# Staging v of three batches through a scratch tensor in HBM, so that its transposes run in float32r

## The chip, the cores and the metric

The kernel runs on one core of a Trainium2 chip. The metric is the device time of one execution in microseconds (us); shown is the median of several runs. One further execution was recorded by the hardware profiler, and all rows below come from it.

## What is computed

The input is four batches of q, k and v, each of 5056 tokens by 256 channels. Attention runs over channels: the score matrix of a batch is 256x256, and its result, 20224 rows of 256, goes through a mixture of eight experts, of which each row takes one.

```python
# attention, one batch
qn = q / (np.linalg.norm(q, axis=1, keepdims=True) + 1e-06)
kn = k / (np.linalg.norm(k, axis=1, keepdims=True) + 1e-06)
a = softmax(kn.transpose(0, 2, 1) @ qn / tau)      # 256 x 256
x = v @ a
# experts, all rows
logits = x @ w_gate + modality_bias[modality_id]
e_idx = np.argmax(logits, axis=1)
h = np.maximum(x[mask] @ w1[e], 0.0)               # 256 -> 1024
out[mask] = gate_w[mask, None] * (h @ w2[e])       # 1024 -> 256
```

## The kernel before

Every float32 product is made of three float32r matmuls: an operand is split into a high part, which is its float32r rounding, and a low part, the rest.

A batch is cut into ten steps of 512 tokens (the last has 448), which makes 40 steps, numbered g = 0 to 39. A step of the main loop (from L726 on) mixes up to three streams of pieces, evenly, by `_interleave` (L20): a block of 512 rows of one expert (`hp` is its first product, L629, and `y` its second, L645; there are blocks from step 7 on), the attention's own stream, and, but for the last batch, the scores of the next batch (`g`, L270 and L274). So the work of about one block, one v step and one score step lies interleaved on every engine.

The attention's stream of step g is `load`, `tr(0)` and `tr(1)` of step g+1, and then `av(0)` to `av(3)` and `route` of step g:

- `load` (L419) takes one of two buffers for v and fills it by a DMA that SyncE issues (L424). Row p of a partition holds four successive tokens.
- `tr(h)` (L434) transposes half of the channels: four TensorE transposes of 128x128 (L440, `vtp`) into one PSUM bank, which ScalarE then copies to the high part `vh` (L444) and VectorE turns into the low part `vl` (L445). v is float32 there, and so are the identity `ident` and the PSUM tile.
- `av(t)` (L447) forms 128 rows of x (L456, `xp`), six matmuls each. `route` (L463) finds each row's expert and scatters the rows by GpSimd into `xs`, a tensor in HBM (L388).

A block loads its rows of `xs` into `xr` (L559) and transposes them by `tr_x` (L605). That one differs from `tr`: `xr` is a float32r tile, filled through a float32 view, and its four transposes (L611, `xtp`) use `identr`, the float32r identity, into a float32r PSUM tile.

Nobody writes an order of engines by hand: the pieces are emitted in the order of the mix, TensorE runs in that order, and on the other engines an instruction whose inputs are ready may be placed ahead of earlier ones. `setup_bias(b+1)` is such a piece: it is emitted after step 5 of a batch, and it begins with two DMAs that load `modi` (L176 and L180), which depend on nothing but a free buffer.

Of the kernel before, what the change touches and what calls it, by code (L numbers as in the profile page):

```python
# [8 lines left out]
F32 = mybir.dt.float32  # L9
F32R = mybir.dt.float32r  # L10
# [3 lines left out]
ALU = mybir.AluOpType  # L14
# [3 lines left out]


def _interleave(*streams):  # L20
    """Emit the pieces of several generators, evenly mixed."""
    lists = [list(s) for s in streams if s]
    total = [len(x) for x in lists]
    at = [0] * len(lists)
    while any(a < n for a, n in zip(at, total)):
        i = min(
            (i for i in range(len(lists)) if at[i] < total[i]),
            key=lambda i: ((at[i] + 0.5) / total[i], i),
        )
        lists[i][at[i]]()  # L30
        at[i] += 1
# [3 lines left out]
def kernel(  # L35
# [13 lines left out]
    nc = tc.nc  # L49
    P = 128  # L50
    B, N, C = q.shape
    T, D = out.shape
    E, _, FF = w1.shape
    TT = 4
    STEP = P * TT
    NS = -(-N // STEP)
    G = B * NS
# [13 lines left out]
    START = 3  # L71
# [6 lines left out]
    p2 = ctx.enter_context(tc.tile_pool(name="p2", bufs=2))  # L78
# [3 lines left out]
    ps1 = ctx.enter_context(tc.tile_pool(name="ps1", bufs=1, space=PSUM))  # L82
    ps2 = ctx.enter_context(tc.tile_pool(name="ps2", bufs=2, space=PSUM))

    # ---- constants
    ident = const.tile([P, P], F32, name="ident")
    make_identity(nc, ident)
    identr = const.tile([P, P], F32R, name="identr")
# [29 lines left out]
    nc.vector.tensor_scalar(desc, iof, -1.0, float(E), ALU.mult, ALU.add)  # L118
    base0 = const.tile([P, E], F32, name="base0")
    nc.vector.tensor_scalar(base0, iof, float(CAP), None, ALU.mult)  # L120
    # the ninth column is the spare region, taken only when no expert has a block left
    eid9 = const.tile([1, E + 1], F32, name="eid9")
    nc.vector.memset(eid9, 0.0)
    nc.vector.tensor_copy(eid9[:, 0:E], iof[0:1, :])
# [10 lines left out]
    nc.vector.memset(end9, float(E * CAP + BLK))  # L135

    xs = dram.tile([ROWS, XW], F32, name="xs")
    pad = const.tile([P, XW], F32, name="pad")
    nc.gpsimd.memset(pad, 0.0)
    nc.gpsimd.memset(pad[:, D + 1 : D + 2].bitcast(I32), BADTOK)  # L140
# [58 lines left out]
        )  # L199
        nc.gpsimd.tensor_tensor(bs, bs, tmp, ALU.add)  # L200

    # ---- scores of one batch, a step of tokens at a time
    gram = {}
    acc = {}
    selfk = {}
# [2 lines left out]
    def kq_pieces(b, s):  # L208
        pp = parts(s)
        st = {}  # L210
# [52 lines left out]
        def mm(h):  # L263
            qs, ks = st[h]
            for t in range(2):
                first = s == 0 and h == 0 and t == 0
                last = s == NS - 1 and h == 1 and t == 1
                for m in range(CH):
                    g = gram[b][m]
                    nc.tensor.matmul(  # L270
                        g, ks[:pp, t, m * P : (m + 1) * P], qs[:pp, t, :],
                        start=first, stop=False, skip_group_check=True,
                    )
                    nc.tensor.matmul(  # L274
                        g[:, 0:C], ks[:pp, t, C + m * P : C + (m + 1) * P], qs[:pp, t, 0:C],
                        start=False, stop=last, skip_group_check=True,
                    )
                    if s < SELF[b]:
                        nc.tensor.matmul(  # L279
                            selfk[b][:, m, :], ks[:pp, t, m * P : (m + 1) * P],  # L280
                            ks[:pp, t, :].rearrange("p (s c) -> p s c", s=2)[:, :, m * P : (m + 1) * P],
                            start=first and m == 0, stop=s == SELF[b] - 1 and h == 1 and t == 1,
                            skip_group_check=True,
                        )
            if s == SELF[b] - 1 and h == 1:
                # the diagonal of k'k, from its high parts with themselves and with the low ones, twice
                dg = p1.tile([P, 2 * P], F32, tag="sc", name=f"dg_{b}", bufs=2)
                normk[b] = p1.tile([P, CH], F32, tag="nk", name=f"nk_{b}")
                for m in range(CH):
                    nc.vector.scalar_tensor_tensor(  # L290
                        dg, selfk[b][:, m, :], 1.0, ident12, ALU.mult, ALU.mult, accum_out=normk[b][:, m : m + 1]
                    )
# [3 lines left out]
            yield lambda h=h: split(h)  # L296
            yield lambda h=h: mm(h)

    # ---- softmax of one batch, and its product with the gate's weights
    attn = {}  # L300

    def softmax_pieces(b):
        st = {}

        def norms():
# [18 lines left out]
            nc.vector.reciprocal(inv, inv)  # L324
            rk = p1.tile([P, CH], F32, tag="rk", name=f"rk_{b}")
            nc.vector.tensor_scalar(rk, inv[:, CH : 2 * CH], small["itau"], None, ALU.mult)
            # 1 / |q| of each column along the free axis, in all partitions
            dq = p1.tile([P, CH, P], F32, tag="at", name=f"dq_{b}")
            for m in range(CH):
                nc.vector.tensor_scalar(dq[:, m, :], ident, inv[:, m : m + 1], None, ALU.mult)  # L330
# [50 lines left out]
            yield lambda m=m: soft(m)  # L381
        yield gate_weights

    # ---- x = v a, its expert, its gate, and its row among the expert's rows
    bases = {}

    def scatter(dst, idx, rows, groups, add, bound, why):
# [16 lines left out]
            )  # L404

    def slots_by(g):
        """Blocks taken by the end of a step: one a step, from the START-th step on."""
        return max(0, g + 1 - START)

    first_block = LAG + START  # L410
# [1 line left out]
    def va_pieces(b, s):  # L412
# [3 lines left out]
        t0 = s * STEP  # L416
        st = {}

        def load():  # L419
            vt = p2.tile([P, TT, C], F32, tag="v", name=f"v_{g}")  # L420
            if pp < P:
                z0 = pp // 32 * 32
                nc.vector.memset(vt[z0:], 0.0)
            nc.sync.dma_start(  # L424
                vt[:pp], v[b, t0 : t0 + pp * TT, :].rearrange("(p t) c -> p t c", t=TT)
            )
            st["v"] = vt
            st["vh"] = p2.tile([P, CH, STEP], F32R, tag="vh", name=f"vh_{g}")
            st["vl"] = p2.tile([P, CH, STEP], F32R, tag="vl", name=f"vl_{g}")
            more = g % 2 == 1 and g + 2 < first_block  # L430
            st["x"] = p3.tile([P, TT, XW], F32, tag="xr" if more else "x", name=f"x_{g}")
            st["L"] = p2.tile([P, TT, E], F32, tag="L", name=f"L_{g}")

        def tr(h):  # L434
            if early and h == 1:
                tp = ps1.tile([P, 512], F32, tag="y1", name=f"vtp_{g}_{h}")
            else:
                tp = ps2.tile([P, 512], F32, tag="h" if early else "aux", name=f"vtp_{g}_{h}")
            for t in range(TT):
                nc.tensor.matmul(  # L440
                    tp[:, t * P : (t + 1) * P], st["v"][:, t, h * P : (h + 1) * P], ident,
                    is_transpose=True, start=t == 0, stop=True, skip_group_check=True,
                )
            nc.scalar.copy(st["vh"][:, h, :], tp)  # L444
            nc.vector.tensor_tensor(st["vl"][:, h, :], tp, st["vh"][:, h, :].bitcast(F32), ALU.subtract)  # L445

        def av(t):  # L447
            ah, al = attn[b]
# [14 lines left out]
        def route():  # L463
# [15 lines left out]
            nc.vector.tensor_tensor(  # L479
                oh.rearrange("p e t -> p t e"), val, vm.unsqueeze(2).to_broadcast(sh), ALU.is_equal  # L480
            )
            # tokens so far of each expert along t, then over the partitions
            W = TT * E
            run_t = p2.tile([P, E, TT], BF16, tag="run", name=f"run_{g}")
            ohf = oh.rearrange("p e t -> p (e t)")
# [38 lines left out]
        return (  # L524
            [load] + [lambda h=h: tr(h) for h in range(CH)],
            [lambda t=t: av(t) for t in range(TT)] + [route],
        )

    # ---- blocks of rows of one expert
    def pick(g, slot, tail):  # L530
        nc.vector.tensor_copy(end9[:, 0:E], bases[g][0:1, :])
        sh = [1, E + 1]
# [23 lines left out]
    def block_pieces(g, slot, pki, tail):  # L556
# [118 lines left out]
                body.append(lambda j=j: m2(j - 1))  # L675
        last = [lambda: m2(NJ - 1)] + [lambda t=t: finish(t) for t in range(TT)]
        if slot == NB_MIN - 1:
            # nothing follows: two of its four tiles of rows are done, and on their way, before the others
            last = [lambda: m2(NJ - 1, range(0, 2)), lambda: finish(0), lambda: finish(1)]
            last += [lambda j=j: m2(j, range(2, 4)) for j in range(NJ - 3, NJ)]  # L680
            last += [lambda: finish(2), lambda: finish(3)]
        return {"slot": slot, "load": prep, "prep": prep2, "first": lambda: m1(0), "body": body, "last": last}

    # ---- program
    def run(pieces):
        for f in pieces:
            f()
# [19 lines left out]
            run(blk[what])  # L707

    def block_stream(blk, nxt):
        """A block behind the end of the one before it, with the next one's preparation in it."""  # L710
        once(blk, "load")
        once(blk, "prep")
        body = list(blk["body"])
        if nxt is not None:
            once(nxt, "load")
            done.add((nxt["slot"], "prep"))
            at = [len(body) * (i + 4) // 8 for i in range(len(nxt["prep"]))]
            for o, f in reversed(list(zip(at, nxt["prep"]))):
                body.insert(o, f)
        before = open_blk[0]["last"] if open_blk[0] is not None else []  # L720
        open_blk[0] = blk
        return [blk["first"]] + before + body

    va = [va_pieces(*divmod(g, NS)) for g in range(G)]
    run(va[0][0])
    for g in range(G):  # L726
        b, s = divmod(g, NS)
        streams = []
# [5 lines left out]
            streams.append(block_stream(blk, waiting[0][1] if waiting and waiting[0][0] <= g - LAG + 1 else None))  # L734
        soft = list(softmax_pieces(b)) if s == 0 and b > 0 else []
        streams.append(soft + (va[g + 1][0] if g + 1 < G else []) + va[g][1])
        if b + 1 < B:
            streams.append(list(kq_pieces(b + 1, s)))
        _interleave(*streams)
# [10 lines left out]
    for _, blk in waiting:  # L750
        once(blk, "load")

    # every count is known: what is left, partial blocks with them
    endi = p1.tile([1, E], I32, tag="endi", name="endi")
    nc.vector.tensor_copy(endi, bases[G - 1][0:1, :])
    for e in range(E):
# [9 lines left out]
        run(block_stream(blk, waiting[0][1] if waiting else None))  # L766
    run(open_blk[0]["last"])

    # what may be left then: up to E - 1 blocks of few rows, and one for each that a step could
    # not take for want of a full one; of those (the counts at the end bound them) there are at most  # L770
    # as many as the steps before the experts are sure to have a full one
    sure = -(-(T - E * (BLK - 1)) // BLK)
    more = NB_MAX - NB_MIN + slots_by(G - 1) - min(sure, slots_by(G - 1))

# [49 lines left out]
```

## Time and profile before

| | |
|---|---|
| median of 3 runs | 1273.65 us (1273.0 to 1274.68) |
| profiled execution, first to last instruction | 1327.4 us |
| its TensorE clock | 0.986 of full speed, mean |
| moved by DMA | 215.33 MB |

The profiled execution is told by its span alone; no other time of it is given. Its span is 53.75 us, or 4.2%, above the median of the runs. So durations from the trace belong to the 1327.4 us and are scaled by 1273.65 / 1327.4 to be set against the median.

PE is TensorE, DVE VectorE, ACT ScalarE, POOL GpSimd, and SPq the queue of SyncE, which issues nearly all DMAs. L424 is line 424 of the kernel before.

### The profile page before, as it was taken

How to read it: one execution, taken by the hardware profiler on the slowest of the kernel's cores; microseconds unless marked ns; L12 is line 12 of the kernel's file. 1: busy time of each engine (PE TensorE's matmuls, PEld its weight loads, DVE VectorE, ACT ScalarE, POOL GpSimd, SP SyncE). 2: the span in 40 equal slices, each digit the busy share in tenths (PEclk: the TensorE clock that was granted, in tenths of full speed). 3: DMA queues.
4: the chain of work that ended last, by engine and by line, in shares of the span. 5: the costliest groups of instructions: out<-in, count | busy, mean ns of one | idle time of the engine just before them, and what ended most of it. 6: DMA issues, size and time to landing. Idle time of an engine off the chain costs nothing.

```text
span 1327.4 us, 24245 instructions
## 1 busy us (share of the span) xinstructions
PE 1254.1 (94%) x8344; PEld 1126.6 (85%) x8344; DVE 869.8 (66%) x2312; ACT 757.6 (57%) x1539; POOL 379.8 (29%) x367
## 2 busy tenths in 40 slices
PE   6987999999999999999999999999999999899994
PEld 5886888888888888888888888988888888799994
DVE  8987976766766766766666776565556655655541
ACT  6765765665655656656565655554555554455451
POOL 6325343132322222222222233322222332212121
PEclk9998999999999999999999999999999999999997
DMA  9556954455555555444554554435444443574400
GB/s 314 179 206 226 280 168 165 144 170 179 170 181 167 161 173 159 158 160 164 180 166 160 159 166 147 134 124 162 150 144 147 146 138 130 161 221 142 144 27 16
DMA packets 113123, 215.33 MB, mean 162 GB/s; under 512 B 16224, under 2 KB 61792, under 8 KB 112992
## 3 DMA queue, kind: packets, MB, share of 16 engines
q1 hardware_dynamic: 97632, 172.11, 41.3%
q0 software_dynamic: 15360, 41.60, 8.3%
q8 instruction: 67, 1.10, 0.3%
q14 instruction: 64, 0.52, 0.1%
HBM read 167.33 MB, written 46.60 MB: 161 GB/s over the span
## 4 chain that ended last, share of the span: by engine, by line
PE 77%; issue 12%; DVE 4%; ACT 2%; DMA 1%; another core or an unknown queue 1%; POOL 1%; SPq 0%; POOLq 0%; ACTq 0%; DVEq 0%
PE y L645 28%; PE hp L629 28%; PE xp L456 9%; PE g L270 4%; PE vtp L440 2%; PE g L274 2%; PE xtp L611 1%; POOL out_dram L388 1%; DMA q<-in_q_dram 1%; DVE ks L246 1%; DVE hl L633 1%; PE selfk L279 0%; ACT hh L632 0%; DVE qs L246 0%
## 5 line engine op out<-in xcount | busy, mean ns | idle before, releaser
L388 POOL DMA_INDIRECT xs<-x,pi x160 | 174.9, 1093 | 691.2 <-ACT w1h L600 495.9
L645 PE MATMUL y<-w2h,hh 128*128 128x256 f32 x1280 | 362.6, 283 | 6.4 <-ACT w1h L600 3.1
L645 PE MATMUL y<-w2h,hl 128*128 128x256 f32 x1280 | 357.8, 280 | 3.9 <-DVE hl L633 2.9
L645 PE MATMUL y<-w2l,hh 128*128 128x256 f32 x1280 | 356.3, 278 | 0.0
L633 DVE SCALAR_TENSOR_TENSOR hl<-hp,hh 128x512 fp32r<-128x512 f32 x320 | 219.7, 687 | 171.1 <-ACT hh L632 159.0
L632 ACT ACTIVATE hh<-hp 128x512 fp32r<-128x512 f32 x320 | 191.5, 598 | 228.1 <-PE hp L629 146.6
L629 PE MATMUL hp<-xh,w1h 128*128 128x512 f32 x640 | 260.1, 406 | 6.6 <-issue 5.9
L645 PEld LDWEIGHTS y<-w2h,hh 128*128 128x128 f32 x1280 | 240.8, 188 | 22.7 <-ACT w1h L600 3.6
L629 PE MATMUL hp<-xl,w1h 128*128 128x512 f32 x640 | 253.5, 396 | 3.0 <-issue 2.4
L629 PE MATMUL hp<-xh,w1l 128*128 128x512 f32 x640 | 253.2, 396 | 1.3 <-issue 1.3
L645 PEld LDWEIGHTS y<-w2l,hh 128*128 128x128 f32 x1280 | 241.9, 189 | 11.1
L645 PEld LDWEIGHTS y<-w2h,hl 128*128 128x128 f32 x1280 | 240.2, 188 | 7.1 <-DVE hl L633 5.6
L388 POOL DMA_INDIRECT out_dram<-yo,xr x160 | 161.9, 1012 | 195.6 <-ACT yo L656 150.4
L601 DVE TENSOR_TENSOR w2l<-w2r,w2h 128x512 fp32r<-128x512 f32 x160 | 110.3, 689 | 68.9 <-ACT w2h L600 66.8
L629 PEld LDWEIGHTS hp<-xh,w1l 128*128 128x128 f32 x640 | 120.7, 189 | 31.0 <-issue 2.9
L629 PEld LDWEIGHTS hp<-xh,w1h 128*128 128x128 f32 x640 | 120.4, 188 | 23.4 <-issue 8.4
L600 ACT CAST w2h<-w2r 128x512 fp32r<-128x512 f32 x160 | 99.4, 621 | 70.8 <-PE y L645 60.5
L629 PEld LDWEIGHTS hp<-xl,w1h 128*128 128x128 f32 x640 | 120.8, 189 | 20.6 <-issue 5.7
L601 DVE TENSOR_TENSOR w1l<-w1r,w1h 128x512 fp32r<-128x512 f32 x160 | 109.9, 687 | 42.4 <-ACT w1h L600 34.3
L600 ACT CAST w1h<-w1r 128x512 fp32r<-128x512 f32 x160 | 99.7, 624 | 53.7 <-PE hp L629 47.0
L270 PE MATMUL g<-qs,ks 128*128 128x512 f32 (+1 forms) x320 | 123.7, 411 | 6.8 <-ACT ks L245 6.4
L456 PE MATMUL xp<-ah,vh 128*128 128x264 f32 x320 | 97.5, 305 | 6.0 <-DVE L L461 3.8
(146 smaller groups left out, 1891.9 us busy)
## 6 DMA issues: line engine op xcount, KB each, us to landing
w1r<-in_moe_w_dram SPq DMA_DIRECT2D x80, 512.0 KB
w2r<-in_moe_w_dram SPq DMA_DIRECT2D x80, 512.0 KB
xr<-xs SPq DMA_DIRECT2D x40, 516.0 KB
v<-in_v_dram SPq DMA_DIRECT2D x36, 512.0 KB
q<-in_q_dram SPq DMA_DIRECT2D x35, 512.0 KB
k<-in_k_dram SPq DMA_DIRECT2D x35, 512.0 KB
xs<-pad SPq DMA_DIRECT2D x9, 516.0 KB
xs<-x,pi POOLq DMA_INDIRECT x160
```

What stands on the lines that cost most here:

```text
L246: nc.vector.tensor_tensor(t[:pp, :, C : 2 * C], st[n][:pp, ts, :], t[:pp, :, 0:C].bitcast(F32), ALU.subtract)
L270: nc.tensor.matmul(g, ks[:pp, t, m * P : (m + 1) * P], qs[:pp, t, :], start=first, stop=False, skip_group_check=True,)
L274: nc.tensor.matmul(g[:, 0:C], ks[:pp, t, C + m * P : C + (m + 1) * P], qs[:pp, t, 0:C], start=False, stop=last, skip_group_check=True,)
L388: ins = nc.gpsimd.indirect_dma_start(out=dst, out_offset=bass.IndirectOffsetOnAxis(ap=idx, axis=0), in_=rows, in_offset=None, bounds_check ...
L440: nc.tensor.matmul(tp[:, t * P : (t + 1) * P], st["v"][:, t, h * P : (h + 1) * P], ident, is_transpose=True, start=t == 0, stop=True, skip ...
L456: nc.tensor.matmul(xp[:, 0:DE], a[:, h, t * P : (t + 1) * P], w[:, h, :], start=i == 0, stop=i == len(seq) - 1,)
L600: nc.scalar.copy(hi, src)
L601: nc.vector.tensor_tensor(lo, src, hi.bitcast(F32), ALU.subtract)
L629: nc.tensor.matmul(hp, w[:, h, fs], x[:, h, :], start=i == 0, stop=i == len(seq) - 1)
L632: nc.scalar.activation(hh, hp, AF.Relu)
L633: nc.vector.scalar_tensor_tensor(hl, hp, 0.0, hh.bitcast(F32), ALU.max, ALU.subtract)
L645: nc.tensor.matmul(y, a[:, tsl], w[:, j % 2, :], start=(j == 0 and i == 0 and t % 2 == 0), stop=(j == NJ - 1 and i == 2), skip_group_check ...
```

## The change

For batches 1 to 3, v is copied word for word to a scratch tensor of the same shape in HBM, `vs1` to `vs3`, by a DMA from HBM to HBM, a step's rows at a time: 27 copies of 512 KB and three of 448 KB, 15.53 MB together (3 x 5056 x 256 words of 4 bytes). `load` then reads from there into a float32r tile, through its float32 view, and `tr` uses `identr` and a float32r PSUM tile, as `tr_x` does. Batch 0 keeps its float32 path.

The copy of a step is a new piece, `stage`, issued by SyncE. It is put into the attention's stream between `tr(0)` and `tr(1)`, from step 6 on: in step g the rows of step g+5 are copied (in step 6 those of steps 10 and 11). With one piece more in that stream, the even mix shifts the others a little: `tr(0)` comes one piece earlier, and each `av` and `route` stands behind the `hp` group of the block that it stood ahead of.

```diff
@@ constants
     xs = dram.tile([ROWS, XW], F32, name="xs")
+
+    vs = [None] + [dram.tile([N, C], F32, name=f"vs{b}") for b in range(1, B)]
@@ va_pieces
+        rows = slice(t0, t0 + pp * TT)
+
+        def stage():
+            nc.sync.dma_start(
+                vs[b][rows, :].rearrange("(p t) c -> p t c", t=TT),
+                v[b, rows, :].rearrange("(p t) c -> p t c", t=TT),
+            )
+
         def load():
-            vt = p2.tile([P, TT, C], F32, tag="v", name=f"v_{g}")
+            vt = p2.tile([P, TT, C], F32R if b > 0 else F32, tag="v", name=f"v_{g}")
+            vf = vt.bitcast(F32) if b > 0 else vt
...
-            nc.sync.dma_start(
-                vt[:pp], v[b, t0 : t0 + pp * TT, :].rearrange("(p t) c -> p t c", t=TT)
-            )
+            src = vs[b] if b > 0 else v[b]
+            nc.sync.dma_start(vf[:pp], src[rows, :].rearrange("(p t) c -> p t c", t=TT))
@@ tr(h)
+            dt = F32R if b > 0 else F32
             if early and h == 1:
-                tp = ps1.tile([P, 512], F32, tag="y1", name=f"vtp_{g}_{h}")
+                tp = ps1.tile([P, 512], dt, tag="y1", name=f"vtp_{g}_{h}")
...
-                    tp[:, t * P : (t + 1) * P], st["v"][:, t, h * P : (h + 1) * P], ident,
+                    tp[:, t * P : (t + 1) * P], st["v"][:, t, h * P : (h + 1) * P], identr if b > 0 else ident,
                     is_transpose=True, start=t == 0, stop=True, skip_group_check=True,
                 )
-            nc.scalar.copy(st["vh"][:, h, :], tp)
-            nc.vector.tensor_tensor(st["vl"][:, h, :], tp, st["vh"][:, h, :].bitcast(F32), ALU.subtract)
+            tf = tp.bitcast(F32) if b > 0 else tp
+            nc.scalar.copy(st["vh"][:, h, :], tf)
+            nc.vector.tensor_tensor(st["vl"][:, h, :], tf, st["vh"][:, h, :].bitcast(F32), ALU.subtract)
@@ main loop
+    staged = NS
     for g in range(G):
...
         streams.append(soft + (va[g + 1][0] if g + 1 < G else []) + va[g][1])
+        while g >= first_block - 1 and staged < min(G, g + NS // 2 + 1):
+            streams[-1].insert(len(soft) + 2, va[staged][2])
+            staged += 1
```

The other lines of the diff only take comments away.

## Rows read from the trace of the kernel before

**Rows 1.** Page, part 1: engine, busy us, share of the span, instructions.

```profile
PE 1254.1 (94%) x8344; PEld 1126.6 (85%) x8344; DVE 869.8 (66%) x2312; ACT 757.6 (57%) x1539; POOL 379.8 (29%) x367
```

**Rows 2.** Page, part 4: the chain that ended last, by engine and by line.

```profile
PE 77%; issue 12%; DVE 4%; ACT 2%; DMA 1%; another core or an unknown queue 1%; POOL 1%; SPq 0%; POOLq 0%; ACTq 0%; DVEq 0%
PE y L645 28%; PE hp L629 28%; PE xp L456 9%; PE g L270 4%; PE vtp L440 2%; PE g L274 2%; PE xtp L611 1%; POOL out_dram L388 1%; DMA q<-in_q_dram 1%; DVE ks L246 1%; DVE hl L633 1%; PE selfk L279 0%; ACT hh L632 0%; DVE qs L246 0%
```

**Rows 3.** Four stretches: length, busy of PE, PEld, DVE, ACT, POOL, clock, DMA share, GB/s.

```profile
74.00:200.00 126.00, 112.84 (x759) 101.41 (x758) 100.65 (x354) 81.16 (x180) 52.89 (x47) 0.95 0.67 210
340.00:650.00 310.00, 301.68 (x2031) 271.99 (x2031) 215.51 (x571) 188.83 (x382) 85.10 (x82) 1.00 0.53 167
650.00:930.00 280.00, 273.13 (x1837) 247.42 (x1837) 179.98 (x494) 158.34 (x323) 75.69 (x72) 0.99 0.47 153
930.00:1147.00 217.00, 213.44 (x1446) 191.66 (x1445) 130.68 (x400) 111.46 (x232) 62.95 (x61) 1.00 0.43 142
```

**Rows 4.** The two lines of transposes: count, busy us, mean ns, idle before.

```profile
L440 PE MATMUL vtp<-ident,v 128*128 128x128 f32 x320 | 49.1, 275 | 6.1 <-DVE pki L547 4.4 <-issue 1.6
L611 PE MATMUL xtp<-identr,xr 128*128 128x128 f32 x320 | 36.7, 237 | 0.0
```

**Rows 5.** Chain in order of time, around two transposes: start us, us, piece.

```profile
150.36 0.29 PE xtp L611 x4
150.65 1.47 PE hp L629 x6
...
165.39 0.44 PE vtp L440 x4
165.83 1.39 PE hp L629 x6
```

**Rows 6.** Waits of PE, whole span: line, releaser, us, times, longest.

```profile
PE hp L629 <- issue: 9.5, 19, 1.0
PE xp L456 <- issue: 8.3, 12, 1.5
```

**Rows 7.** DMA: packets, MB and engine share of SyncE's queue; the whole; v's loads.

```profile
q1 hardware_dynamic: 97632, 172.11, 41.3%
DMA packets 113123, 215.33 MB, mean 162 GB/s; under 512 B 16224, under 2 KB 61792, under 8 KB 112992
v<-in_v_dram SPq DMA_DIRECT2D x36, 512.0 KB
```

**Rows 8.** Line L424: ns of an issue on SyncE's queue, first and last start.

```profile
L424 SPq DMA_DIRECT2D v<-in_v_dram x40: 327/339/422, 33.0 to 1039.9; - x40
```

**Rows 9.** Timeline of SyncE's queue, four stretches: start us, us, issue.

```profile
63.62 0.38 SPq L231 DMA_DIRECT2D k<-in_k_dram  x1
...
70.28 0.48 SPq L176 DMA_DIRECT2D modi<-in_moe_modality_id_dram  x1
...
74.04 0.39 SPq L231 DMA_DIRECT2D k<-in_k_dram  x1
85.14 0.33 SPq L424 DMA_DIRECT2D v<-in_v_dram  x1
...
178.41 0.38 SPq L176 DMA_DIRECT2D modi<-in_moe_modality_id_dram  x1
...
616.62 0.34 SPq L424 DMA_DIRECT2D v<-in_v_dram  x1
```

**Rows 10.** Timeline of PE: the transposes that use the last of these loads.

```profile
673.25 0.60 PE L440 MATMUL vtp<-ident,v 128*128 128x128 f32 x4
```

**Rows 11.** Chain in order of time, three places where it left the engines.

```profile
63.62 4.50 DMA k<-in_k_dram
...
170.99 7.42 issue
...
178.84 2.57 DMA modi<-in_moe_modality_id_dram
```

More of the change, by code (lines that the diff above doesn't have):

```diff
@@ L417, in va_pieces @@
         st = {}
+        rows = slice(t0, t0 + pp * TT)
[4 more added lines that the diff above has]
+            )
         def load():
-            vt = p2.tile([P, TT, C], F32, tag="v", name=f"v_{g}")
+            vt = p2.tile([P, TT, C], F32R if b > 0 else F32, tag="v", name=f"v_{g}")
+            vf = vt.bitcast(F32) if b > 0 else vt
             if pp < P:
                 z0 = pp // 32 * 32
-                nc.vector.memset(vt[z0:], 0.0)
-            nc.sync.dma_start(
-                vt[:pp], v[b, t0 : t0 + pp * TT, :].rearrange("(p t) c -> p t c", t=TT)
-            )
+                nc.vector.memset(vf[z0:], 0.0)
+            src = vs[b] if b > 0 else v[b]
+            nc.sync.dma_start(vf[:pp], src[rows, :].rearrange("(p t) c -> p t c", t=TT))
             st["v"] = vt
@@ L434, in tr @@
         def tr(h):
+            dt = F32R if b > 0 else F32
             if early and h == 1:
-                tp = ps1.tile([P, 512], F32, tag="y1", name=f"vtp_{g}_{h}")
+                tp = ps1.tile([P, 512], dt, tag="y1", name=f"vtp_{g}_{h}")
             else:
-                tp = ps2.tile([P, 512], F32, tag="h" if early else "aux", name=f"vtp_{g}_{h}")
+                tp = ps2.tile([P, 512], dt, tag="h" if early else "aux", name=f"vtp_{g}_{h}")
             for t in range(TT):
                 nc.tensor.matmul(
-                    tp[:, t * P : (t + 1) * P], st["v"][:, t, h * P : (h + 1) * P], ident,
+                    tp[:, t * P : (t + 1) * P], st["v"][:, t, h * P : (h + 1) * P], identr if b > 0 else ident,
                     is_transpose=True, start=t == 0, stop=True, skip_group_check=True,
                 )
-            nc.scalar.copy(st["vh"][:, h, :], tp)
-            nc.vector.tensor_tensor(st["vl"][:, h, :], tp, st["vh"][:, h, :].bitcast(F32), ALU.subtract)
+            tf = tp.bitcast(F32) if b > 0 else tp
+            nc.scalar.copy(st["vh"][:, h, :], tf)
+            nc.vector.tensor_tensor(st["vl"][:, h, :], tf, st["vh"][:, h, :].bitcast(F32), ALU.subtract)
         def av(t):
@@ L526, in va_pieces @@
             [lambda t=t: av(t) for t in range(TT)] + [route],
+            stage,
         )
```

## The prediction, written before the result

> **What bounds the kernel now.** I read the page's shares first. TensorE is busy 94% of the span, VectorE 66%, and no other engine near it [rows 1]. The chain that ended last says the same by time: 77% of it is TensorE's, most of that `hp` and `y`, and DMA has 1% [rows 2]. A share over the whole span hides stages, so I then read stretches: in the three that cover most of batches 1 to 3, TensorE is busy 97 to 98% at a clock of 0.99 to 1.00, while the DMA engines are about half idle (0.53, 0.47, 0.43) [rows 3]. Between 74 and 200 us, where the blocks of experts begin, it is otherwise: TensorE 112.84 of 126.00 us, and DMA at 0.67 [rows 3]. So where the change removes work, work on TensorE is what counts, and where it adds work, DMA, there is room, unless the added transfers gather where there is little.
>
> The little idle time that TensorE has is put down to "issue" for the most part: 9.5 us in 19 waits before `hp`, 8.3 us in 12 before `xp` [rows 6]. I keep that in mind for a rival.
>
> **The change part by part.** *What is removed.* Two groups of four transposes in each of 30 steps go from float32 to float32r: 60 groups, 240 of the 320 in line L440. The trace has both kinds. One transpose is shown with 275 ns against 237 [rows 4], but TensorE's instructions overlap, so what counts is when the next can go. The chain has the two kinds ahead of the same work: float32r 0.29 us and then `hp` 1.47, float32 0.44 and then `hp` 1.39 [rows 5]. The float32r group is shorter by 0.15, but 0.08 of that comes back in the first matmuls behind it; together 1.76 against 1.83 us, so a group saves 0.07 us. I take 0.07; the bounds are 0 (all of it comes back) and 0.15 (none does). 60 x 0.07 = 4.2 us of 1327.4 us, and scaled to the median 4.0; by the bounds 0 and 60 x 0.15 = 9.0, scaled 8.6. TensorE is the bound in those stretches [rows 3], so all of it should reach the end.
>
> A rule speaks for more. The Trainium skill, FP8 and Floating Point Precision, section TensorE Precision Notes, says that true float32 takes four passes through the array. By it a float32r group would take a quarter of the float32 one, and the change would save 60 x 0.44 x 3/4 = 20 us, an estimate; the rows with 0.44 against 0.29 [rows 5] are far from four to one, so for transposes I go by the rows.
>
> *What is added: 30 copies.* SyncE spends about 0.34 us to issue one [rows 8], 10 us in all on a queue that is not on the chain (0% in [rows 2]): nothing. The transfer: SyncE's queue moved 172.11 MB in 41.3% of the span [rows 7], that is 548 us of all 16 engines, 3.19 us for a MB. 15.53 MB then take 49.5 us, 1.65 us for one copy. The trace has no transfer from HBM to HBM; the lower bound is that of a load, 1.65 us, the upper twice that, if reading and writing count each. At one copy per step of some 31 us, even 3.3 us fit into the half of the time in which the DMA engines are idle [rows 3]. What hides it: the slack of the loads. The v load issued at 616.62 [rows 9] is, by its count, the one used at 673.25 [rows 10], 57 us later. Without that cover a load behind a copy would be late by the copy, 1.65 us, and each such case on the path costs as much.
>
> *What is added: a wait.* A v load now waits for its copy, on SyncE, and behind it stand the loads of weights, xr, q and k. The copy is emitted in the fourth step before the transposes that use it, the load goes out some two steps before, so the copy has about two steps, 60 us, to take 2 to 4 us. Nothing is waited for. I take 0; upper bound, if one load per step is late by a copy, is the 49.5 us.
>
> *What moves.* `tr(0)` goes one piece forward; each `av` and `route` falls behind an `hp` group of 1.4 us [rows 5]. That makes the scatters to `xs` later by 1.4 us once per step, and they are read by blocks at least a step later: 0. The same number of matmuls stands on TensorE in another order: 0, with the rival below. ScalarE and VectorE read PSUM through a float32 view, with the same shapes: 0.
>
> **The sum.** -4.2 + 0 + 0 + 0 = -4.2 us on a span of 1327.4, so 1273.65 - 4.0 = 1269.7 us.
>
> **Rival 1, slower: the copies go out early and in a heap.** They depend on nothing, and on SyncE such an instruction need not keep its place: a load of `modi` that is emitted half way through batch 2, after step 25, went out at 178.41 us, when the kernel was in batch 0 [rows 9]. It even stood on the chain, with 7.42 us of issue ahead of it and 2.57 us of DMA [rows 11]. SyncE has gaps, as from 74.04 to 85.14 [rows 9]: 11 us, in which 30 issues of 0.34 us fit. The place is then the first 200 us. There a wait for a load was already on the chain: `k`, issued at 63.62, 4.50 us [rows 9, 11]. Between 74 and 200 us the DMA engines are free for 0.33 x 126 = 41.6 us, and 49.5 us of copies leave 7.9 that don't fit [rows 3]; scaled, 7.6, which gives 1269.7 + 7.6 = 1277.3 us. If all 30 went into that one gap, the load at 85.14 would stand behind 49.5 - 11.1 = 38 us of copies, and 1306 us is the upper bound. Against it speaks that most loads of that time have cover too, and that a `modi` load shows only one instruction's early start, not thirty. It decides as soon as more than 4.2 + 2.7 = 6.9 us of copies, a little over four of the thirty, are waited for. The Trainium skill, DMA: Bandwidth & Descriptors, section Issuing engines are not separate DMA queues, says that all DMAs end on the same 16 engines and interleave, which is how a copy could delay loads here; no row of before shows such a delay.
>
> **Rival 2, no change.** Two to three copies waited for (3.3 to 5 us) eat the 4.0; or the stops called issue, about half a microsecond each [rows 6], set the pace of a step, and the 0.14 us saved in it is given back there. 1272 to 1276 us, middle 1273.7.
>
> **Rival 3, much faster.** The new order takes away the stops: 17.8 us of them are in [rows 6]. Half of it would be 8.5 us scaled: 1261 us. No row says that they hang on the place of `av` or `tr`, so it has little chance. Or a float32r group takes but a quarter of the float32 one's 0.44 us [rows 5]: 60 x 0.33 = 19.8 us, scaled 19.0, and 1254.7 us; the 0.29 us that the same rows show for it leave this almost no chance.
>
> **How the numbers follow.** I give the forecast 0.40, more than forecast by the order 0.07, by a group of a quarter 0.02, no change 0.21, and the heap 0.30. A difference under 0.2%, 2.5 us, could not be told from none here; the forecast's 4.0 us is over that, but not by much. Faster is then 0.40 + 0.07 + 0.02 = 0.49, same 0.21, slower 0.30. The likeliest is 1269.7 us; its own range is 1265 (the bound of 8.6) to 1271. The range of all goes from 1264, below which lie rival 3's two cases (0.09), to 1287, half way or so from 1269.7 to rival 1's upper bound, above which I leave 0.08.
>
> **What the profile after would show.** Right: in line `vtp` of batches 1 to 3 a mean near 237 ns, and chain pieces of 0.29 us; 27 + 3 issues of `vs` on SyncE, and 215.33 + 15.5 = 231 MB (a copy counted once); the stretches of batches 1 to 3 shorter by 0.14 us per step and TensorE as busy as before; no DMA on the chain there. Rival 1 would show most issues of `vs` before 200 us, a DMA share near 1 there, and chain pieces of DMA or waits for loads between 60 and 200 us. Rival 2 shows transposes as forecast with stretches of unchanged length; rival 3 fewer waits for issue. Wrong would be the forecast if the copies are late and v loads wait on them, which shows as waits of `vtp` for a DMA.

## The result and the profile after

The changed kernel takes 1277.14 us (median of 16 runs), the one before 1274.23 us beside it (16 runs): a ratio of 1.0022, 95% interval 1.0015 to 1.0028. It is slower by 2.9 us, where 4.0 us less had been forecast.

The page of the changed kernel: shares (as [rows 1]), the chain by engine and line (as [rows 2]), and SyncE's queue and the bytes (as [rows 7]).

```profile
PE 1232.0 (97%) x8344; PEld 1116.2 (88%) x8344; DVE 866.6 (68%) x2312; ACT 752.4 (59%) x1539; POOL 385.2 (30%) x367
...
DMA packets 114083, 230.86 MB, mean 181 GB/s; under 512 B 16704, under 2 KB 62272, under 8 KB 113472
...
q1 hardware_dynamic: 98592, 187.64, 46.0%
...
PE 88%; issue 3%; DMA 3%; DVE 2%; ACT 1%; POOL 1%; SPq 0%; POOLq 0%; ACTq 0%; DVEq 0%
```

230.86 - 215.33 = 15.53 MB: the thirty copies are there. But the span is 1275.3 us, 52 us below that of [rows 1 to 11], and "issue" has 3% of the chain where it had 12%. That is no work of the change. The same program takes 1274 us on some chips and 1312 to 1335 us on others, where TensorE stops for about 1 us in each step. The profile ahead of the prediction, with its span of 1327.4 us and its waits named issue, looks like one from a chip of the second kind. Below, the two are called chips without and with stops. Part of what that profile showed of the first 130 us is seen on such chips alone, so from here on the kernel with the shifted mix and nothing else (run e9, on a chip without stops, ratio 0.9993) stands in for the kernel before.

The transposes, grouped by line, as [rows 4]; then two places of the changed kernel's chain, as [rows 5]:

```profile
L451 PE MATMUL vtp<-identr,v 128*128 128x128 f32 x240 | 27.5, 237 | 0.0
L451 PE MATMUL vtp<-ident,v 128*128 128x128 f32 x80 | 12.3, 274 | 0.0
```

```profile
93.19 10.16 DMA xs<-x,pi
...
104.60 1.69 PE xp L468 x6
...
316.27 0.29 PE vtp L451 x4
316.57 1.46 PE hp L642 x6
```

The transposes do what was forecast of them: 237 ns, and 0.29 + 1.46 us in place of 0.44 + 1.39 [rows 5]. The earlier place is new: a scatter issued at 93.19 us landed 10.16 us later, and six `xp` matmuls, 0.73 us elsewhere in this chain, took 1.69 behind it. The landings of the scatters issued between 88 and 95 us, as far as the trace has them, in the changed kernel and then in e9:

```profile
DMA to landing us min/median/max: 6.8/8.6/10.4
```

```profile
DMA to landing us min/median/max: 3.4/3.9/4.7
```

Two timelines of the changed kernel show what lay beside these scatters: the issues of copies on SyncE's queue (start, duration, count), and GpSimd's scatters around the gap.

```profile
75.64 2.67 SPq L424 DMA_DIRECT2D vs<-in_v_dram  x3
...
86.71 1.12 SPq L424 DMA_DIRECT2D vs<-in_v_dram  x2
...
91.86 1.12 SPq L424 DMA_DIRECT2D vs<-in_v_dram  x2
...
97.08 1.86 SPq L424 DMA_DIRECT2D vs<-in_v_dram  x3
...
211.10 2.40 SPq L424 DMA_DIRECT2D vs<-in_v_dram  x4
```

```profile
98.30 0.97 POOL L390 DMA_INDIRECT xs<-x,pi  x1 [0.30 <-ACT x L472]
104.46 0.97 POOL L390 DMA_INDIRECT xs<-x,pi  x1 [5.18 <-ACT qs L247]
```

Ten copies go out between 75.64 and 99 us, the other twenty between 143 and 213.5 us; none is left for the steps in whose pieces they stand. The waits of the changed kernel between 92 and 108 us (waiting instruction, releaser, us, times, longest):

```profile
DVE pi L520 <- DMA xs<-x,pi: 5.6, 1, 5.6
PE xp L468 <- DVE L L473: 5.3, 1, 5.3
...
ACT x L526 <- DMA xs<-x,pi: 5.2, 1, 5.2
```

VectorE may not write the row indices `pi`, nor ScalarE the tokens' numbers in `x`, until an earlier scatter is through with the buffer. Behind `pi` on VectorE stands `L`, which takes the gate's part out of PSUM, and TensorE waits for it with `xp`. Three stretches of 4 us, columns as in [rows 3], first of the changed kernel, then of the shifted mix without copies (e9):

```profile
96.00:100.00 4.00, 3.28 (x26) 2.83 (x25) 1.63 (x6) 2.14 (x5) 2.67 (x3) 1.00 0.93 307
100.00:104.00 4.00, 0.00 (x0) 0.00 (x0) 0.53 (x3) 0.55 (x2) 0.00 (x0) 0.67 1.15 373
104.00:108.00 4.00, 3.40 (x14) 3.20 (x15) 3.30 (x15) 1.45 (x5) 2.94 (x3) 0.50 0.65 252
```

```profile
96.00:100.00 4.00, 4.00 (x34) 3.74 (x33) 3.56 (x21) 2.63 (x10) 2.92 (x3) 1.00 0.61 194
100.00:104.00 4.00, 4.00 (x33) 3.67 (x32) 3.99 (x23) 2.84 (x9) 3.04 (x4) 1.00 0.58 206
104.00:108.00 4.00, 4.00 (x32) 3.47 (x31) 3.70 (x28) 2.60 (x7) 3.08 (x4) 1.00 0.70 234
```

With the copies the DMA engines are at 0.93 and 1.15, TensorE stands still from 100 to 104 us, and then it is busy but at a granted clock of 0.50 (1.2 of 2.4 GHz) and gets 14 matmuls done where the other kernel gets 32. Without copies DMA is at about 0.6 and TensorE never stops. The Trainium skill, DMA: Bandwidth & Descriptors, section Issuing engines are not separate DMA queues, says that DMAs started by ScalarE, SyncE or GpSimd run on the same 16 engines and interleave; the trace agrees, as GpSimd's scatters landed after 8.6 us (median) beside SyncE's copies and after 3.9 without them.

Where the time went can then be read block by block, from the first and the last start of the blocks' transposes (line by its forms: count, min/median/max ns, first to last start), in the changed kernel and in e9:

```profile
L624 PE MATMUL xtp<-identr,xr x320: 222/244/282, 130.5 to 1227.5; 128*128 128x128 f32 x160
```

```profile
L621 PE MATMUL xtp<-identr,xr x320: 222/244/281, 122.8 to 1225.5; 128*128 128x128 f32 x160
```

The first starts differ by 7.7 us, the last by 2.0. The first scatter had gone out 1.75 us earlier in the changed kernel (88.93 us, against 90.68 in e9), so from there to the first block it loses 9.4 us. A second slow stretch belongs to that: between 124 and 128 us its clock is 0.50, and 1.00 in e9. The first rows that are transposed in float32r come only at 193.54 us:

```profile
193.54 0.46 PE L451 MATMUL vtp<-identr,v 128*128 128x128 f32 x4
```

So the loss ahead of the first block is the copies' alone: neither the mix, which e9 has too, nor the float32r transposes can have a part in it. After it, over 27 steps from block 6 to block 33 (the timeline of TensorE, the same transposes of these two blocks, changed kernel and e9):

```profile
305.07 0.46 PE L624 MATMUL xtp<-identr,xr 128*128 128x128 f32 x4
...
1088.65 0.46 PE L624 MATMUL xtp<-identr,xr 128*128 128x128 f32 x4
```

```profile
299.25 0.46 PE L621 MATMUL xtp<-identr,xr 128*128 128x128 f32 x4
...
1086.60 0.46 PE L621 MATMUL xtp<-identr,xr 128*128 128x128 f32 x4
```

783.58 against 787.35 us: 3.77 us less, 0.14 us per step, and TensorE has no wait there in either kernel. So theory 3 of the next section falls: the transposes do give what was forecast.

### The profile page after: what moved, and what is told of

It is laid out like the page before. It is cut to its first block, busy times and chain, and to the rows that moved or that the text cites. A ratio compares the mean times of both kernels' runs of the same rounds, so it can differ in the third digit from the quotient of the medians.

```text
span 1275.3 us, 24243 instructions
## 1 busy us (share of the span) xinstructions
PE 1232.0 (97%) x8344; PEld 1116.2 (88%) x8344; DVE 866.6 (68%) x2312; ACT 752.4 (59%) x1539; POOL 385.2 (30%) x367
## 2 busy tenths in 40 slices
DMA packets 114083, 230.86 MB, mean 181 GB/s; under 512 B 16704, under 2 KB 62272, under 8 KB 113472
## 4 chain that ended last, share of the span: by engine, by line
PE 88%; issue 3%; DMA 3%; DVE 2%; ACT 1%; POOL 1%; SPq 0%; POOLq 0%; ACTq 0%; DVEq 0%
PE hp L642 34%; PE y L658 34%; PE xp L468 9%; PE g L272 4%; PE g L276 2%; PE vtp L451 2%; PE xtp L624 2%; DMA xs<-x,pi 1%; DMA q<-in_q_dram 1%; DMA k<-in_k_dram 1%; DVE ks L248 1%; DVE qs L248 1%; DMA w1r<-in_moe_w_dram 0%; PE ns L313 0%; PE selfk L281 0%
## 5 line engine op out<-in xcount | busy, mean ns | idle before, releaser
L390 POOL DMA_INDIRECT xs<-x,pi x160 | 172.2, 1076 | 649.4 <-issue 458.6
L390 POOL DMA_INDIRECT out_dram<-yo,xr x160 | 169.9, 1062 | 187.5 <-ACT yo L669 141.8
L468 PE MATMUL xp<-ah,vh 128*128 128x264 f32 x320 | 94.4, 296 | 8.8 <-DVE L L473 5.3
```

The costliest lines, as they stand in the source:

```text
L390: ins = nc.gpsimd.indirect_dma_start(out=dst, out_offset=bass.IndirectOffsetOnAxis(ap=idx, axis=0), in_=rows, in_offset=None, bounds_check ...
L468: nc.tensor.matmul(xp[:, 0:DE], a[:, h, t * P : (t + 1) * P], w[:, h, :], start=i == 0, stop=i == len(seq) - 1,)
```

## The experiments

Theory 1: the copies, out early and in a heap, cost 6 to 7 us, and the transposes give 4. Theory 2: the shifted mix costs that. Theory 3: the transposes give nothing, and the copies cost 3. Ratios are against the kernel before on the same chip. Chips without stops: e9, e10, e18 (1274 us before); with stops: all others (1318 to 1327).

**The kernel before again (e1, e5).**

> The kernel before, unchanged, for a second profile: its first profiled execution took 53 us more than its timed runs, with stops of TensorE that the changed kernel's profile does not have. If those stops were an accident of that execution, the span here is near 1272 us, TensorE is busy about 97% of it, and no wait named issue is left. If they belong to the order of the kernel before, the span is near 1327 us again.

> The kernel before once more, for a profile beside the runs of this call. The chip of the runs so far in this study took 1319 us for it, with a stop of about 1 us in every step, and the one on which the changed kernel was compared took 1274. If this call's chip is of the second kind: span near 1272, steps of 29.84 us (the changed kernel's 29.70 and 0.14 for its two transpose groups), no waits named issue. If it is of the first kind: span near 1318 and steps of 30.9.

1320.81 and 1324.79 us, spans 1319.0 and 1323.0, and waits named issue, on two chips with stops (1319.19 and 1326.84 us in their other runs). So the stops are not an accident of one execution. They go with the chip; as each chip was seen in one set of runs only, what in it makes them stays open. The early stretch on such a chip, without any copy (e5):

```profile
96.00:100.00 4.00, 2.31 (x12) 1.69 (x12) 1.11 (x9) 0.37 (x2) 1.95 (x2) 0.60 0.28 99
100.00:104.00 4.00, 3.74 (x16) 3.55 (x17) 2.90 (x13) 2.77 (x8) 1.01 (x2) 0.55 0.45 131
```

TensorE stops and loses its clock there with DMA at 0.28. On such a chip the first scatters pause anyway (97.3, then 102.7 us in e5). That the early copies therefore have little left to spoil is argued, not shown.

**The shifted mix alone (e2, e6, e9).**

```diff
         def stage():
-            nc.sync.dma_start(
-                vs[b][rows, :].rearrange("(p t) c -> p t c", t=TT),
-                v[b, rows, :].rearrange("(p t) c -> p t c", t=TT),
-            )
+            return
-            vt = p2.tile([P, TT, C], F32R if b > 0 else F32, tag="v", name=f"v_{g}")
+            vt = p2.tile([P, TT, C], F32, tag="v", name=f"v_{g}")
-            src = vs[b] if b > 0 else v[b]
+            src = v[b]
-            dt = F32R if b > 0 else F32
+            dt = F32
```

> The new piece stands where stage stands, but it is empty: float32 transposes, v loaded from the input, no copies, only the shifted mix of the pieces. Theory 1 (the copies, issued in a heap before 215 us, cost about 7 us and the float32r transposes give 4): 1274, ratio 1.000. Theory 2 (the shifted order costs the 7 us, and the copies nothing): 1281, ratio 1.0055. Theory 3 (float32r transposes give nothing, and the copies cost 3): 1274, ratio 1.000.

> The shifted mix alone, again: an empty piece, float32 transposes, no copies. Theory 1 (copies in a heap cost 7, transposes give 4, the order nothing): ratio 1.000. Theory 2 (the order costs: it lengthens the step in which a batch ends by 4 to 6 us, as it did on the chip of the first call): ratio 1.005 to 1.006 on either chip. Where the chip has no stops there is also nothing that the new order could relieve.

> The shifted mix alone (an empty piece, float32 transposes, no copies), a third time, because the two chips so far had stops of about 1 us per step in the kernel before (1319 and 1327 us) that the changed kernel's own profile does not show (1277). If this chip takes 1274 for the kernel before: theory 1 (the copies cost, the order nothing) says 1.000; theory 2 (the order costs) says 1.005, as 7 us are needed to turn -4 into +3. If it is a chip with stops: 1.006 to 1.013 again.

1326.05 us, ratio 1.0060 (1.0039 to 1.0082); 1345.03, ratio 1.0127 (1.0106 to 1.0149); and without stops 1274.03, ratio 0.9993 (0.9984 to 1.0002). So theory 2 falls for chips without stops, where the change was measured, and the mix is a cost of its own on those with stops. It falls where a batch ends. The stretch with the softmax of batch 3 on the second of these chips, by the chain of e6:

```profile
870.68 1.49 issue
872.17 0.97 PE y L655 x6
873.14 2.39 PE hp L639 x6
```

Six `hp` matmuls take 2.39 us in place of 1.40 after such a stop. The step that holds it took 39.7 us there against 32.0 in e5. Why the new mix meets the stops more badly there was not settled. It is not worse everywhere: by the starts of the blocks' transposes an ordinary step took about 30.3 us in e2 and 31 in e1 on the same chip, so the new mix did relieve stops there, while the steps in which batches 2 and 3 start their softmax grew by 4 and 6 us.

**The copies alone (e3, e13, e16).** As the diff above, but `stage` keeps its copy, which nobody reads.

> The copies are made in their place, but nobody reads them: float32 transposes, v loaded from the input. Theory 1: copies cost 7, nothing is given back: 1281, ratio 1.0055. Theory 2: 1281 too, but equal to the run with the order alone. Theory 3: as the changed kernel, 1277, ratio 1.0022.

> The copies in the changed kernel's place, unread, with float32 transposes. Theory 1: on a chip without stops 1274 + 6.5 = 1280.5, ratio 1.005. Theory 3: as the changed kernel, 1277, ratio 1.002.

> The unread copies with float32 transposes once more, for a chip without stops: theory 1 says 1280.5, ratio 1.005; theory 3 says 1277, ratio 1.002. If the chip is one with stops: 1.004 to 1.006 again, which the shifted order alone explains there.

1324.21 us, ratio 1.0041 (1.0022 to 1.0060); 1327.55, 1.0062 (1.0039 to 1.0084); 1327.08, 1.0059 (1.0033 to 1.0084). All three ran on chips with stops. On the one where the mix alone was run too (e2, 1.0060) it gives as much: no cost of the copies is seen there; for e13 and e16 there is no such partner. So the copies alone were never timed on a chip without stops. That they are the loss there is read from the traces, since the first float32r transposes start after it.

**The changed kernel with the old mix (e7, e10).**

```diff
-            streams[-1].insert(len(soft) + 2, va[staged][2])
+            streams[-1][len(soft) + 1] = lambda f=streams[-1][len(soft) + 1], c=va[staged][2]: (f(), c())
```

> The changed kernel with its copies and float32r transposes, but each copy is issued in the piece of the transposes ahead of it, so that the mix is that of the kernel before. Theory 1: the copies are as crowded as in the changed kernel, so 1277 on a chip without stops, ratio 1.002. Theory 2: the order was the cost, the 4 us of the transposes show: 1270, ratio 0.997.

> The changed kernel with the mix of the kernel before. On a chip of 1274 us theory 1 says 1.002 (copies as crowded as in the changed kernel), theory 2 says 0.997 (the transposes' 4 us remain). On a chip with stops: 1.0005 again, since the stops take back what the transposes give.

With stops 1327.62 us, ratio 1.0005 (0.9986 to 1.0024). Without, 1277.66 us, ratio 1.0026 (1.0015 to 1.0038): as the changed kernel, though the mix is that of before. The order is not the loss on a chip without stops. The late scatters are there again: those issued between 88 and 95 us landed after 6.1 to 10.8 us.

**A ring of five steps as scratch (e4, e8, e14).** Five copies go early, then one per step.

```diff
-    vs = [None] + [dram.tile([N, C], F32, name=f"vs{b}") for b in range(1, B)]
+    vs = [dram.tile([STEP, C], F32, name=f"vs{i}") for i in range(5)]
-                vs[b][rows, :].rearrange("(p t) c -> p t c", t=TT),
+                vs[g % 5][0 : pp * TT, :].rearrange("(p t) c -> p t c", t=TT),
```

> The changed kernel, but the scratch holds five steps and is used in a ring: a copy writes where the load of five steps before has read, so five copies can go early, and then one goes per step. Same bytes, same mix of pieces, same transposes. Theory 1: the crowding is gone, and the 4 us of the transposes show: 1270 to 1271, ratio 0.997. Theory 2: no change against the changed kernel, 1277. Theory 3: copies cost nothing when spread, transposes give nothing: 1274, ratio 1.000.

> The changed kernel with its scratch as a ring of five steps, so that all but five copies go one per step; the mix is the changed kernel's. Theory 1: ratio 0.997. Theory 2: as the changed kernel, 1.002 on a chip without stops. On the chip of the first call it gave 1.0043.

> The ring of five steps: five copies before 100 us and not ten, then one per step. Theory 1, if each early copy costs alike: half of 6.5, 1274 + 3.2 - 4.2 = 1273, ratio 0.999; if only those count that lie beside the first scatters, from 88 us on: 1270, ratio 0.997. Rival (any copy beside the first blocks costs): 1277.

1324.55 us, ratio 1.0043 (1.0022 to 1.0063); 1342.14, 1.0118 (1.0089 to 1.0147); 1326.75, 1.0052 (1.0027 to 1.0078). All on chips with stops, each near what the mix alone gives (1.0060 and 1.0127 on the chips of the first two; on the third it was not run). They tell nothing on how many early copies it takes.

**Copies that wait for scatters (e11, e12).**

```diff
+            after(ins.ins, written[max(first_block - 1, g - NS // 2) - 1])
```

> The changed kernel, but each copy has to wait for the scatters of the step before the one that issues it, so that none goes before about 125 us; afterwards one goes per step. Theory 1, as the traces now have it (on a chip without stops the ten copies that go out before 100 us make the first block start 6 to 7 us later, the twenty others cost nothing, and the transposes give 0.14 us per step): 1274 - 4.2 = 1270, ratio 0.9967, and the transposes of the first block's rows end near 124 us. Theory 3 (the transposes give nothing): 1274, ratio 1.000. Rival to theory 1: any copy that lies beside the first blocks costs, early or not: 1276, ratio 1.002. On a chip with stops the shifted order weighs more than all this: 1.004 to 1.012.

> As the paced copies, but with the mix of the kernel before. Theory 1: as with the shifted mix on a chip without stops, 1270, ratio 0.9967; on a chip with stops 0.999 to 1.000, since the stops take back what a step saves. Theory 3: 1.000 on both.

1352.53 us, ratio 1.0251 (1.0227 to 1.0275), and 1376.19, ratio 1.0400 (1.0364 to 1.0436), the latter with the mix of before. Theory 1's number was missed by far, for another reason than the one under test. The waits of SyncE's queue in e11, the row of the copies' line:

```profile
SPq L424 <- DMA xs<-x,pi: 70.8, 10, 12.9
```

While a copy waits, up to 12.9 us, the loads behind it on SyncE stand too: between 178.37 and 191.24 us the queue issued nothing. A wait was the wrong way to place them. That these pauses make up the whole loss is likely, but no run separates it from the rest.

**Copies behind the blocks' loads, without a wait (e15, e17, e18).** The mix is that of before (as in e7 and e10); each copy is only ordered on SyncE behind the latest load of a block's rows.

```diff
+            tc.add_manual_dep(
+                ins.ins, xloads[-1].name,
+                mybir.DependencyInfo(mybir.DependencyClass.NoSync, mybir.DependencyReason.DATA),
+                reason="behind the block's load, on SyncE",
+            )
...
+            xloads.append(ins.ins)
             st["xr"] = xr
```

> The changed kernel with the mix of the kernel before, and each copy is placed on SyncE's queue behind the latest load of a block's rows, in program order and without a wait on anything else. So no copy goes before about 121 us, then one or two per step, and SyncE does not stand still for them as it did with the paced copies. Theory 1 (the early place of ten copies costs 6 to 7 us, the transposes give 0.14 us per step): on a chip without stops 1270, ratio 0.9967, first block as early as with no copies. Theory 3 (transposes give nothing): 1.000. Rival (copies beside the first blocks cost as well): 1.002. On a chip with stops: 0.998 to 1.000.

> The copies behind the blocks' loads, none before about 121 us, with the mix of the kernel before, again, for a chip without stops. Theory 1 (the ten early copies cost 6 to 7 us, all others nothing, the transposes give 0.14 us per step): 1270, ratio 0.9967, interval below 1; the 4 us windows between 96 and 108 us keep a busy TensorE at full clock, and the steps take 29.70 us. Rival (copies beside the first blocks cost as well, wherever they are): 1.000 to 1.002. Theory 3 (transposes give nothing): 1.000 and steps of 29.85. If the chip has stops: 0.998 to 1.003, which tells nothing new.

> The copies behind the blocks' loads once more, the last run, for a chip without stops. Theory 1 (the ten early copies are the whole loss): 1270, ratio 0.9967, full clock between 96 and 108 us, steps of 29.70 us. Rival (copies beside the first blocks cost as well): 1.000 to 1.002. Theory 3 (transposes give nothing): 1.000 and steps of 29.85. On a chip with stops: about 1.000, and the question stays open.

With stops 1319.33 us, ratio 1.0004 (0.9975 to 1.0033), and 1327.51, ratio 1.0001 (0.9982 to 1.0020). Without, 1272.11 us, ratio 0.9979 (0.9969 to 0.9989): 0.2% faster than the kernel before, where the changed kernel was 0.2% slower. From e10 to e18, which ran on two chips without stops and differ by the place of the copies (and, as shown below, of a k load), 1.0026 became 0.9979, 6.0 us of 1274. The stretches of e18 that stood still in the changed kernel:

```profile
100.00:104.00 4.00, 4.00 (x33) 3.67 (x32) 3.94 (x22) 2.84 (x8) 3.07 (x4) 1.00 0.60 217
104.00:108.00 4.00, 4.00 (x31) 3.45 (x30) 3.84 (x28) 2.56 (x7) 3.09 (x4) 1.00 0.67 218
```

TensorE is busy throughout at full clock. The first and the last block's transposes in e10 and in e18:

```profile
L624 PE MATMUL xtp<-identr,xr x320: 222/238/257, 131.9 to 1229.6; 128*128 128x128 f32 x160
```

```profile
L631 PE MATMUL xtp<-identr,xr x320: 222/238/257, 123.4 to 1225.0; 128*128 128x128 f32 x160
```

The first block starts 8.5 us earlier than in e10, 0.6 us behind e9 (122.8). But the last is ahead by 4.6 us only. The difference lies between the first two blocks, where three of the moved copies now go (two at 117.74, one at 130.12 us); the chain of e18 there:

```profile
129.63 10.29 DMA k<-in_k_dram
...
143.08 2.56 PE y L665 x12
```

A k load took 10.29 us, and 12 `y` matmuls behind it 2.56 in place of 1.40. So 0.9967, theory 1's number, was just missed. This is not shown to be a cost of the copies beside the first blocks, because the edit moved more than them. The q load and this k load on SyncE's queue, in e9 and then in e18:

```profile
120.05 0.35 SPq L233 DMA_DIRECT2D q<-in_q_dram  x1
120.51 0.61 SPq L233 DMA_DIRECT2D k<-in_k_dram  x1
```

```profile
121.73 0.69 SPq L233 DMA_DIRECT2D q<-in_q_dram  x1
...
129.63 0.43 SPq L233 DMA_DIRECT2D k<-in_k_dram  x1
```

In e18 the k load stands behind the next loads of weights and rows and goes out 9 us later, as it does in e15 and e17 (13 and 11 us behind its q load). It does not take longer: in e9, without any copy, it landed after 10.0 us. So the late issue is enough for the wait, and whether copies beside the first blocks cost anything stays open. This profiled execution was the slowest of the 11 (1274.34 us); the fastest took 1268.69.

## Why the prediction was wrong

**What bounds the kernel.** Right for the steps of batches 1 to 3: a saving on TensorE reached the end undiminished on a chip without stops.

**The transposes, 4.2 us.** Right: 0.14 us per step over 27 steps, as 2 x 0.07. The rule of four passes (the Trainium skill, FP8 and Floating Point Precision, section TensorE Precision Notes) did not hold for these transposes: 0.44 against 0.29 us.

**The copies, 0.** This is the step that failed: "At one copy per step of some 31 us, even 3.3 us fit". They did not go at one per step; thirty went in 138 us, ten of them before the first block, at a cost of 6 to 9 us (first block 7.7 us late here, 9.4 from the first scatter on, 8.5 from e18 to e10; 6.0 by the times, 1.0026 against 0.9979). The forecast took the place in the code for the place in time, though the early `modi` load of rival 1 [rows 9] said the contrary. This was the fact to weigh most: what waits for nothing can be issued long before the code around it.

**Rival 1.** The right mechanism, with 1277.3 us forecast and 1277.14 measured, but the working behind the 7.9 us was not what happened, so that the two numbers agree is luck. The copies that filled the DMA engines most, twenty between 143 and 213 us, cost nothing that shows: changed kernel and e9 are 6.4 us apart at block 1 and 6.1 at block 4. What cost was among the ten that lie about the scatters of steps 0 to 2: late scatters stopped VectorE, then TensorE, and then the clock fell. Which of the ten it takes was not shown, and that the twenty were harmless because blocks keep TensorE busy is argued only. It was scatters of GpSimd, not a load queued behind the copies on SyncE as the rival had it.

**The wait of v loads, 0.** Right: the changed kernel has no wait of TensorE for a v load.

**The order, 0.** Right without stops (0.9993), wrong with them (1.006 and 1.0127). The changed kernel itself was not run on a chip with stops.

**Rival 2** by stops that take the saving back: it fits the chips with stops, where e7, e15 and e17 gave 1.0005, 1.0004 and 1.0001, but it is not shown. In e7's trace the stretch from block 1 to block 2 took 35.3 us, and 29.9 in e5 on the same chip, so there at least a loss stands against the saving. **Rival 3** did not occur: without stops there was nothing to relieve, and on the chip of e2, where the mix relieved ordinary steps, the ends of batches cost more.

**The base.** A span 4.2% above the median was scaled away, when it should have made the stops themselves suspect: the early rows (a clock of 0.95, scatters late without copies) were, as the later runs suggest, those of another chip than the one timed.

## What to carry to other kernels

A DMA that depends on nothing has no place of its own: it can go long before the code around it, as all thirty did here, and the fit of its bytes has to be checked where it really goes, above all against transfers that free small buffers. To move it, order it behind another issue of the same queue, and look at what else changes its place there; a wait on that queue holds up the loads behind it. And when a profile's span does not agree with the timed runs, the rows that explain the difference are not rows of the kernel that is timed.

## What the runs showed of the hardware

The same kernel takes 1274 us on some chips and 1318 to 1327 us (medians) on others; the steps of batches 1 and 2 are 29.85 us long in e9 and about 31 in e5, and the difference is stops of TensorE of about 1 us. Their cause was not found. The stop of the changed kernel cost twice: TensorE did no matmul from 100 to 104 us, and from 104 to 108 us its granted clock was 0.50 (1.2 GHz). A copy from HBM to HBM of 512 KB took SyncE 0.49 us or more to issue where a load took 0.33, and its median time to landing was 7.5 us in the heap and 5.4 us in e18, where the copies go one per step, against 4.4 us for the changed kernel's v loads from the scratch.
